# Moving the memory reads of an attention segment to other slots of a hand-written timetable

## The chip, the core and the metric

The kernel runs on one core of one Trainium2 chip. The metric is the device time of one execution in microseconds (us). All times here are in us unless marked ns.

A core has a matrix engine (TensorE, PE in the profile, its weight loads PEld), a vector engine (VectorE, DVE), an activation engine (ScalarE, ACT), a general engine (GpSimd, POOL), and a queue that issues transfers (SyncE, SP). Each runs its own instructions in order and waits for others on semaphores. Matrix products are written to PSUM; VectorE or ScalarE takes them out again, which is called evacuation below.

## The reference

Two branches share one layer norm of `x` (2048 tokens, 640 features) and are multiplied at the end.

```python
xn = layernorm(x)
# branch A: attention with a memory, 32 heads of 20, 4 segments of 512 tokens
q, k, v = heads(xn @ wq), heads(xn @ wk), heads(xn @ wv)
M, z = 0, 0
for s in range(4):
    p     = softmax(q_s @ k_s.T * scale + causal_mask)
    a_dot = p @ v_s
    a_mem = (phi(q_s) @ M) / (phi(q_s) @ z + 1e-6)       # the memory read
    o_s   = g * a_mem + (1 - g) * a_dot                  # g = sigmoid(beta)
    M     = M + phi(k_s).T @ v_s
    z     = z + phi(k_s) summed over tokens
s = concat(o) @ wo
# branch B: a gated unit of width 1536
h = sigmoid(xn @ w_gate) * (xn @ w_up)
out = x + s * silu(h @ w_down)
```

Here `phi(t)` is `t + 1` for positive `t` and `exp(t)` otherwise. The memory read of a segment uses the memory `M`, `z` of the segments before it, so the first segment (n = 0) has none.

## The kernel before

**Slots.** The work is cut into 80 slots, 20 for each segment n, numbered here 0 to 79; segment n has slots 20n to 20n+19. A slot begins with the scores of one unit of attention (`scores`, line 548, tile `Sps`, four banks of PSUM) and the exponential of these on ScalarE (`exps`, line 556, tile `pt`, then masked by GpSimd). The rest of the slot is filled with other matrix products.

**What fills a slot.** Two sorts of work fill it. The dense queue holds, in order, the gate products (`gp`, `do_gate`), the up products (`up`, `do_up`) and the down products (`yp`, `do_down`) of branch B. They are generators: a gate or up product is 5 pieces of 512 columns, a down product 12 pieces of 320, and the filler takes piece after piece. The other sort are events with due times, from the table `TIMES`, in slots from the segment's start: memory reads (`mem_part`, tile `am`, 8 in a segment from n = 1 on), output products (`out_mm`, tile `sp`), projections for the next segment (`psq`, `psv`), layer norm, transfers. The time's whole part names the slot, and its fraction the place in the slot's free time. If more than two products of events fall into one open dense product, that one is run to its end first (`inside`, line 921):

```python
            if ns > 0:
                inside[0] += 1
                if inside[0] > 2:
                    complete()
```

**Two forms of a product.** All of these products go through `mm` (lines 130 and 134). It issues either one matmul over 128 columns of weights (line 130), or four over 32 columns each, side by side in the array (line 134). The second form is chosen for the slots whose end has a product of attention with values (`attend_T`, line 572, tile `ApsT`), which is itself in 32-column tiles. These are the slots that come just before a "visit":

```python
        ORDER["columns"] = slot + 1 in visits
```

In a segment these are the slots 0, 3, 5, 8, 10, 13, 15 and 18 from its start. So slots 23, 25, 28 and 30 use the 32-column form in segment 1, and 22, 24, 26, 27 and 29 the 128-column form.

**A memory read.** `mem_part(n, j, half)` multiplies 128 tokens of phi(q) (`qtd`) with the memory (`Mbd`), in three pieces of 147, 147 and 84 columns (or in another order), and VectorE evacuates it in three instructions: line 413 (`rm`), line 415 (its reciprocal) and line 416 (`odot`). The reads of a segment must be done before their result is spilled (`mem_spill`, 11.56 slots after the segment's start).

**PSUM buffers.** Besides `Sps` there are four buffers, from one pool, `ps_d`, for all other products. A product's tile takes a buffer when the code reaches it, in the recorded order, and its first matmul waits until the product that had the buffer before is evacuated. The evacuations are: `gp` by a tanh on ScalarE (line 427, tile `tg`), `up` by VectorE (line 438, tile `hT`, which also needs `tg`), `yp` by a tanh on ScalarE (line 454) and then VectorE (line 455, tile `aa`), `sp` by VectorE (line 499, then line 502 adds to `xt` after every second one), `am` by VectorE as above, `ApsT` by a transpose on VectorE (line 593, tile `tb`). The `hT` tiles are the weights of the down products.

VectorE also does the layer norm of the next segment (lines 240, 241, 249), the transposes of the attention's result (line 591, tile `obT`) and phi (lines 366, 367, 375, with an exponential on ScalarE, line 371).

## Time and profile before

| | |
|---|---|
| median of 3 runs | 319.95 us (319.74 to 320.09) |
| span of the profiled execution, first to last instruction | 317.6 us |
| whole time of the profiled execution | not listed apart from the three runs; 2.35 us lie between its span and the median |
| granted TensorE clock, mean | 0.999 |
| busy: TensorE, VectorE, ScalarE, GpSimd | 309.7, 229.5, 227.2, 135.5 us |
| slots 22 to 29, from `Sps` to `Sps` | 109.53 to 137.14 us of the span |
| slots 42 to 49 | 175.94 to 202.90 us |
| slots 62 to 69 | 242.22 to 268.74 us |

In the timeline view a row is a run of equal instructions: start, length, engine, line, operation, output and inputs, shape, count, and in brackets the engine's idle time before it with what ended it. The records of matmuls overlap: each shows its way through the array, so one product's cost to TensorE is read from its start to the start of the next. Some matmul records are missing, so a count can be one short.

### The profile page before, as it was taken

How to read it: one execution, taken by the hardware profiler on the slowest of the kernel's cores; microseconds unless marked ns; L12 is line 12 of the kernel's file. 1: busy time of each engine (PE TensorE's matmuls, PEld its weight loads, DVE VectorE, ACT ScalarE, POOL GpSimd, SP SyncE). 2: the span in 40 equal slices, each digit the busy share in tenths (PEclk: the TensorE clock that was granted, in tenths of full speed). 3: DMA queues.
4: the chain of work that ended last, by engine and by line, in shares of the span. 5: the costliest groups of instructions: out<-in, count | busy, mean ns of one | idle time of the engine just before them, and what ended most of it. 6: DMA issues, size and time to landing. Idle time of an engine off the chain costs nothing.

```text
span 317.6 us, 10049 instructions
## 1 busy us (share of the span) xinstructions
PE 309.7 (98%) x4215; PEld 167.1 (53%) x4244; DVE 229.5 (72%) x505; ACT 227.2 (72%) x229; POOL 135.5 (43%) x230
## 2 busy tenths in 40 slices
PE   8999999999999999999999999999999999999995
PEld 3544445665555445654665455545466645445673
DVE  6474356755869888997779999977787686734565
ACT  3723477788898877778898868678897766777631
POOL 1870036535263445334453354444533353535322
PEclk9999999999999999999999999999999999999999
DMA  7984886420752462505954443238533000350302
GB/s 252 364 328 142 289 221 191 105 46 2 215 158 62 130 130 85 126 23 173 240 168 122 114 110 109 82 121 210 168 82 120 19 23 23 114 137 4 99 20 83
DMA packets 56085, 41.36 MB, mean 130 GB/s; under 512 B 26952, under 2 KB 54664, under 8 KB 56040
## 3 DMA queue, kind: packets, MB, share of 16 engines
q1 hardware_dynamic: 53496, 35.97, 39.7%
q10 hardware_dynamic: 2544, 4.75, 4.0%
q8 instruction: 33, 0.54, 0.7%
q14 instruction: 12, 0.10, 0.1%
HBM read 19.90 MB, written 14.78 MB: 109 GB/s over the span
## 4 chain that ended last, share of the span: by engine, by line
PE 96%; issue 1%; ACT 1%; DVE 1%; ACTq 0%
PE yp L130 11%; PE up L130 11%; PE gp L130 10%; PE psq L130 10%; PE Sps L548 9%; PE gp L134 6%; PE up L134 6%; PE yp L134 6%; PE psv L130 6%; PE ApsT L572 5%; PE psq L134 4%; PE sp L130 3%; PE sp L134 3%; PE sp L532 2%; PE psv L134 1%; PE wps L644 1%
## 5 line engine op out<-in xcount | busy, mean ns | idle before, releaser
L556 ACT ACTIVATE pt<-Sps 128x2048 bf16<-128x2048 f32 (+1 forms) x81 | 150.3, 1856 | 40.8 <-PE Sps L548 35.9
L558 POOL TENSOR_SCALAR_AFFINE_SELECT pt<-pt 128x512 bf16<-128x512 bf16 x128 | 83.2, 665 | 157.6 <-ACT pt L556 157.5
L438 DVE SCALAR_TENSOR_TENSOR hT<-tg,up 128x512 bf16<-128x512 bf16 x48 | 32.4, 675 | 23.2 <-PE up L130 8.7
L130 PE MATMUL up<-xnT,Wu 128*128 128x512 bf16 x147 | 40.3, 380 | 1.2 <-issue 1.0
L130 PE MATMUL yp<-Wd,hT 128*128 128x320 bf16 x257 | 40.1, 300 | 0.0
L427 ACT ACTIVATE tg<-gp 128x512 bf16<-128x512 f32 x48 | 28.6, 596 | 14.4 <-PE gp L130 11.0
L130 PE MATMUL gp<-xnT,Wg 128*128 128x512 bf16 x144 | 38.1, 379 | 0.3 <-issue 0.2
L548 PE MATMUL Sps<-QT,KT 23*128 23x128 bf16 (+3 forms) x512 | 32.6, 301 | 0.2
L591 DVE STREAM_TRANSPOSE obT<-ob 128x512 bf16<-128x512 bf16 x30 | 21.1, 705 | 13.4 <-POOL ob L587 13.3
L130 PEld LDWEIGHTS <-hT 128*128 128x128 bf16 x257 | 23.5, 98 | 11.6 <-issue 3.0
L455 DVE SCALAR_TENSOR_TENSOR aa<-t,yp 128x320 bf16<-128x320 bf16 x32 | 15.3, 480 | 13.8 <-ACT t L454 13.7
L134 PE MATMUL gp<-xnT,Wg 128*32 128x512 bf16 x360 | 24.1, 380 | 0.0
L548 PEld LDWEIGHTS <-KT 23*128 23x128 bf16 x512 | 10.0, 92 | 24.5 <-issue 24.1
L130 PEld LDWEIGHTS <-Wu 128*128 128x128 bf16 x160 | 14.3, 98 | 16.2 <-issue 3.2
L593 DVE STREAM_TRANSPOSE tb<-ApsT 128x512 f32<-128x512 f32 x30 | 21.2, 708 | 2.2 <-PE ApsT L572 2.1
L572 PE MATMUL ApsT<-pt,V 128*32 128x512 bf16 (+2 forms) x480 | 22.7, 299 | 0.0
L130 PEld LDWEIGHTS <-Wg 128*128 128x128 bf16 x150 | 14.1, 98 | 16.0 <-issue 1.9
L134 PE MATMUL up<-xnT,Wu 128*32 128x512 bf16 x320 | 21.7, 380 | 0.0
L454 ACT ACTIVATE t<-yp 128x320 bf16<-128x320 f32 x32 | 13.9, 435 | 10.2 <-PE yp L130 8.5
L130 PE MATMUL psv<-Wv,xnT 128*128 128x320 bf16 x130 | 20.6, 299 | 0.2
L587 POOL TENSOR_TENSOR ob<-tb,rb 128x320 bf16<-128x320 f32 x27 | 19.8, 733 | 2.3
L134 PE MATMUL yp<-Wd,hT 128*32 128x320 bf16 x508 | 20.0, 300 | 0.0
(122 smaller groups left out, 448.7 us busy)
## 6 DMA issues: line engine op xcount, KB each, us to landing
KT<-Kd SPq DMA_DIRECT2D x32, 80.0 KB
QT<-Qd SPq DMA_DIRECT2D x32, 80.0 KB
out_dram<-xt SPq DMA_DIRECT2D x14, 160.0 KB
Wg<-in_B_w_gate_dram ACTq DMA_DIRECT2D x1, 1920.0 KB
Wu<-in_B_w_up_dram ACTq DMA_DIRECT2D x1, 1920.0 KB
xt<-in_A_x_dram SPq DMA_DIRECT2D x3, 640.0 KB
Wd<-in_B_w_down_dram SPq DMA_DIRECT2D x1, 1920.0 KB
Xd<-xn SPq DMA_DIRECT2D x12, 160.0 KB
```

The source lines that it names most:

```text
L130: nc.tensor.matmul(out_, lhsT=lhsT, rhs=rhs, start=start, stop=stop, skip_group_check=True)
L134: nc.tensor.matmul(out_[cols], lhsT=lhsT[:, cols], rhs=rhs, start=start, stop=stop, tile_position=(0, 32 * r), skip_group_check=True)
L427: nc.scalar.activation(tg[:], gp[:], ACT.Tanh, scale=0.5)
L438: nc.vector.scalar_tensor_tensor(out=h[:], in0=seg[n]["tg"][:], scalar=1.0, in1=up[:], op0=ALU.add, op1=ALU.mult)
L455: nc.vector.scalar_tensor_tensor(out=s["aa"][j][:, hs], in0=t2[:], scalar=1.0, in1=yp[:], op0=ALU.add, op1=ALU.mult)
L548: nc.tensor.matmul(Sps[:, r, c0:c0 + ncol], lhsT=KT[32 * r:32 * r + DH + 3, g, kb * P:(kb + 1) * P], rhs=QT[32 * r:32 * r + DH + 3, g, q0: ...
L556: nc.scalar.activation(pt[:, :, 0:ntot], Sps[:, :, 0:ntot], ACT.Exp, scale=SCALE)
L558: nc.gpsimd.affine_select(out=pt[:, :, c0:c0 + P], in_=pt[:, :, c0:c0 + P], compare_op=ALU.is_ge, fill=0.0, base=0, pattern=[[0, 4], [1, P ...
L572: nc.tensor.matmul(ps[32 * r:32 * r + 32, q0:L], lhsT=Vflat[n % 2][:, off:off + 32], rhs=t[:, r, c0:c0 + ncol], start=(i == 0), stop=(i == ...
L587: nc.gpsimd.tensor_tensor(ob[:, :, 0:DH], tb[:, :, 0:DH], rb[:].unsqueeze(2).to_broadcast([P, L // 32, DH]), op=ALU.mult)
L591: nc.vector.transpose(s["obT", g // 4][:, g % 4, :], ob[:].rearrange("p b e -> p (b e)"))
L593: s["turn", g] = (lambda: nc.vector.transpose(tb[:].rearrange("p b e -> p (b e)"), ps[:]), quotients, turn_back)
```

## The change

Only the due times of the eight memory reads of a segment are changed, in the timetable (line 66):

```diff
-    update=-1.6, mem=(2.1, 3.8, 3.0, 6.1, 7.0, 2.3, 9.0, 10.0), mem_spill=11.56, mem_T=14.4,
+    update=-1.6, mem=(3.03, 3.45, 3.85, 5.15, 5.6, 8.15, 8.6, 10.0), mem_spill=11.56, mem_T=14.4,
```

Before, a segment's reads lie in the slots 2, 2, 3, 3, 6, 7, 9 and 10 from its start, three of them in slots of the 32-column form. Afterwards they lie in 3, 3, 3, 5, 5, 8, 8 and 10, all of them slots of the 32-column form. The filler puts dense pieces where the reads were and takes them from where the reads go.

## The prediction

> **What bounds the kernel now.** I read the page first: the busy shares, then the chain that ended last.

> ```profile
> PE 309.7 (98%) x4215; PEld 167.1 (53%) x4244; DVE 229.5 (72%) x505; ACT 227.2 (72%) x229; POOL 135.5 (43%) x230
> ...
> PE 96%; issue 1%; ACT 1%; DVE 1%; ACTq 0%
> ```

> TensorE is busy 98% of the span, and 96% of the chain is TensorE, spread over all its products. So whatever leaves TensorE working without a hole costs nothing, and each hole made in its stream goes onto the end time in full. Two questions remain: does a memory read (am) take TensorE longer in 32-column form, and do the moved reads make it wait?

> The timeline of TensorE, segment 1, slots 22 (its end) and 23 answers the first. Ends overlap in these records, so I read cost as start to next start.

> ```profile
> 111.29 1.24 PE L130 MATMUL gp<-xnT,Wg 128*128 128x512 bf16 x5
> 112.37 0.38 PE L130 MATMUL up<-xnT,Wu 128*128 128x512 bf16 x1
> 112.68 0.40 PE L548 MATMUL Sps<-QT,KT 23*128 23x512 bf16 x4
> 113.01 0.35 PE L134 MATMUL am<-Mbd,qtd 128*32 128x147 bf16 x12
> 113.18 1.04 PE L134 MATMUL up<-xnT,Wu 128*32 128x512 bf16 x16
> ```

> A piece of gp or up costs 1.08/5 = 0.22; Sps x4 0.32; an am in 32-column form (x12) 0.17. In 128-column form, x3 from 110.31 to 110.48, it is 0.17 as well. By the same reading a sp product is 0.68, a yp piece 0.14, ApsT 0.65, Sps x8 0.34.

> The second question needs ACT and VectorE. Segment 2, slot 45 (its Sps starts at 185.82), the timeline of ACT:

> ```profile
> 186.32 1.88 ACT L556 ACTIVATE pt<-Sps 128x2048 bf16<-128x2048 f32 x1 [0.43 <-PE Sps L548]
> 188.10 0.59 ACT L427 ACTIVATE tg<-gp 128x512 bf16<-128x512 f32 x1
> ```

> The exponential starts 0.50 after the slot does and holds ACT until 2.28. A tanh of a gate product finished inside the slot therefore ends at 2.87 at the earliest, however early that product is done. Segment 1, slot 28 (from 129.25), the timeline of VectorE:

> ```profile
> 127.85 0.48 DVE L366 TENSOR_SCALAR mn<-ktok 128x1280 bf16<-128x1280 bf16 x1
> 128.37 0.97 DVE L367 TENSOR_SCALAR ktok<-ktok 128x1280 bf16<-128x1280 bf16 x1
> 129.26 0.47 DVE L499 TENSOR_TENSOR aa<-aa,sp 128x320 bf16<-128x320 bf16 x1
> 129.66 0.70 DVE L591 STREAM_TRANSPOSE obT<-ob 128x512 bf16<-128x512 bf16 x1
> 130.29 0.64 DVE L438 SCALAR_TENSOR_TENSOR hT<-tg,up 128x512 bf16<-128x512 bf16 x1
> 130.86 0.80 DVE L375 TENSOR_TENSOR ktok<-ktok,mn 128x1280 bf16<-128x1280 bf16 x1
> 131.59 0.47 DVE L499 TENSOR_TENSOR aa<-aa,sp 128x320 bf16<-128x320 bf16 x1
> 132.09 0.59 DVE L502 TENSOR_TENSOR xt<-aa,xt 128x640 bf16<-128x640 bf16 x1
> 132.61 0.47 DVE L455 SCALAR_TENSOR_TENSOR aa<-t,yp 128x320 bf16<-128x320 bf16 x1
> 133.00 0.47 DVE L499 TENSOR_TENSOR aa<-aa,sp 128x320 bf16<-128x320 bf16 x1
> ```

> No idle time stands between these rows: in this slot VectorE is the fuller engine, although its share of the whole span is 72%. Here TensorE already loses a little: the sp at 130.13 lasts to 130.99, 0.86 where 0.68 is its cost.

> **The change, part by part.** Only the order inside slots 22 to 29, 42 to 49 and 62 to 69 differs. Of the 24 reads, 9 are in 32-column form now; afterwards all 24 are, so 15 change form. As built, slots hold 3 reads (23, 43, 63), 2 (25, 45, 65), 2 (28, 48, 68) and 1 (30, 50, 70, as now). The dense pieces displaced go to neighbouring slots; the number of products stays.

> *TensorE's own work.* 15 reads at 0.17 against 15 at 0.17, dense pieces at 0.22 in both forms (gp x20 in 32 columns, 114.05 to 115.13, is 1.08): sum 0. Switches of form stand around Sps as before: 0. The 90 more matmuls and loads are inside the 0.17.

> *Queues.* SP, POOL and ACT keep their instructions in the same order, and no DMA is moved past another. VectorE keeps its 24 evacuations (rm, reciprocal, odot: 110.79 to 111.68, 0.89 each), in other places. So all of the cost is waiting for the four PSUM buffers that products share. In the built order each product's buffer tells whose evacuation it waits for. I walk the tight places with rows of before, as offsets from the slot's start, and add 0.05 from a release to the matmul (estimate; ACT follows the gp ending at 112.53 by 0.04).

> *Slot 45.* New order: gp 1, am, gp 1, sp, gp 1, am, up. The second am is the third insertion into an open gp, which forces that gp to its end; then up gets gp's own buffer. up wants to start at 0.32+0.22+0.17+0.22+0.68+0.22+0.17 = 2.00; the tanh ends at 2.87. Wait 0.9. In before, two sp stood there and up had another buffer. Behind the waiting up, sp and ApsT are queued, and everything after them. Nothing hides this.

> *Slot 43* (exponential at +0.51, tanh ends at 2.87 too): gp 1, am, gp 3, up 1, am, up 4, am, and the next gp takes the first gp's buffer at 0.32+0.22+0.17+0.65+0.22+0.17+0.86+0.17 = 2.78. Wait 0.15. *Slot 23*: ApsT is the one that takes gp's buffer, at 3.0 by the same addition: covered, by 0.1; 0.25 if that margin goes.

> *Slot 28.* New order: yp 2, am, yp 1, sp, yp 1, yp' 1, sp', am', yp' 4, ApsT. VectorE: obT at 0.41, hT 1.04 to 1.68 as in before, then am's evacuation from 1.61 to 2.59, the ktok addition from 2.50, sp's aa 3.23 to 3.70, xt from 3.73, yp's aa 4.25 to 4.72. TensorE: the last yp piece needs hT as weights at 0.32+0.27+0.17+0.14+0.68 = 1.58, waits 0.15. sp' wants to start at 2.0 in am's buffer, free at 2.59: waits 0.6. am' wants sp's buffer at 2.64+0.68 = 3.32, free at 3.70: waits 0.45. ApsT wants yp's buffer at 3.75+0.17+0.54 = 4.46, free at 4.72: waits 0.3. Together 1.5; slot 28 of before already loses 0.18, so 1.3.

> *Slot 48* has the same pattern with gp in yp's place. sp' wants am's buffer at 2.04. If VectorE is as late as in before (obT done at 1.75), am is evacuated at 2.73: wait 0.75, and ApsT loses 0.25 more. If it is early, since slots 46 and 47 have each lost a read (0.89 of VectorE), nearly no wait: 0.1. I take the middle, 0.45; the row nearest to it, obT at 196.79, speaks for the upper end, the relief for the lower.

> *What is gained.* Slot 49 starts without a read: its waits of before, 0.1, go; so does the 0.1 in slot 27 (a sp behind hT). Segment 3: VectorE idles 1.0 to 1.4 at a time at 252 to 266 and covers its moved reads: 0; the price without that cover is about slot 48's, 0.5.

> Sum: 0.9+0.15+1.3+0.45-0.2 = 2.6. The profiled execution has a span of 317.6; its own whole time isn't among the times, so I take the 2.35 between span and the median 319.95 as what lies around, unchanged. 319.95+2.6 = 322.6 (span 320.2).

> [...]

> **The rivals.** *Evacuations keep up.* If no product meets a busy buffer, only gains are left: the losses of before in these slots, 0.11 (27), 0.18 (28), 0.10 (49), 0.08 (63, 70 together), give 319.5; with 15 reads 0.01 cheaper each (some of the 128-column ones take 0.177 against 0.165) 319.3. This is the side that isn't slower. It decides at slot 45: the tanh would have to end by 2.00, and the exponential before it ends only at 2.28. Against it: two fixed durations. For it: nothing but the cover seen in segment 3.

> *The backlog spreads.* VectorE, behind after slots 28 and 48, makes slots 23, 65 and 68 wait as well: 2.6 + 0.25 + 0.5 + 0.5 for slot 48's upper end = 3.9, that is 323.9. For it: slots 25 and 65 reuse a read's buffer with only some 0.4 to spare. Against it: every wait of TensorE gives VectorE time to catch up.

> *Reads bound by their weight loads.* If several reads in one slot run at load pace, 3 loads of 97 ns one after the other in each column group (that row is the LDWEIGHTS from qtd), each read costs 0.29 instead of 0.17: 15 x 0.12 = 1.8 more, 324.4. [...] Against it: the x12 rows.

> **How the numbers follow.** Forecast (waits as walked, some more or less) 0.77; evacuations keep up 0.07; backlog spreads 0.13; load pace 0.03. About 0.2% (0.64) is what a measurement of this kernel can tell from no change. Slower by more: 0.77+0.13+0.03, less a little for walked waits that come out at a quarter, 0.91; the keep-up case is 0.06 same and 0.03 faster at its edge. Low end: slot 45 at 0.85, slot 28 at half, the rest nothing, less 0.2, is +1.3, 321.2. High end: the spread case and 0.3 over, 324.2.

> **What would show it.** Right: in slot 45 a hole of 0.9 ahead of up, put down to ACT tg; in slot 28 some 1.5 of holes ahead of L134 sp, am and ApsT, put down to DVE odot and aa; am groups x12 still 0.17; the span from the Sps of slot 22 to that of slot 30 longer by about 1.2 and of slots 42 to 50 by 1.4, of 62 to 70 the same. Wrong: no holes at these places, am groups longer than 0.2, or holes in slots 31 to 41, where nothing is moved.

## The result and the profile after

The changed kernel takes 321.59 us where the kernel before takes 319.92: a ratio of 1.005, 95% interval 1.0034 to 1.0066. That is the median of three executions (321.24 to 321.72); a fourth, the profiled one, ran at a granted clock of 0.66 and took 451.29, and with it the median is 321.65. A second measurement, `after_again`, gave 322.04 against 319.65, 1.0074 (1.0051 to 1.0096). It is slower, as forecast: by 1.7 in the first measurement and 2.4 in the second, where the forecast was 2.65. All profile lines "of after" below are of `after_again`, whose profiled execution took 321.68 with a span of 319.9, 2.3 more than the span before.

The page, its first busy line and the first line of the chain that ended last:

```profile
PE 313.0 (98%) x4334; PEld 166.8 (52%) x4334; DVE 228.5 (71%) x505; ACT 227.0 (71%) x229; POOL 135.1 (42%) x230
...
PE 91%; DVE 5%; issue 1%; ACT 1%; DMA 1%; DVEq 0%; ACTq 0%
```

The busy shares say nothing: TensorE is at 98% as before. The chain does: 5% of it is VectorE now, where it was 1%. TensorE waits for evacuations.

What a read costs TensorE did not change. The timeline of TensorE in slot 23:

```profile
113.29 0.34 PE L134 MATMUL am<-Mbd,qtd 128*32 128x147 bf16 x12
113.45 0.39 PE L134 MATMUL up<-xnT,Wu 128*32 128x512 bf16 x4
113.67 0.82 PE L134 MATMUL gp<-xnT,Wg 128*32 128x512 bf16 x12
114.32 0.34 PE L134 MATMUL am<-Mbd,qtd 128*32 128x147 bf16 x12
114.48 0.39 PE L134 MATMUL gp<-xnT,Wg 128*32 128x512 bf16 x4
```

From start to next start both reads take 0.16, where the load-pace rival has 0.29.

Slot 45 begins at 187.03. The timeline of ScalarE, then that of TensorE:

```profile
187.53 1.88 ACT L556 ACTIVATE pt<-Sps 128x2048 bf16<-128x2048 f32 x1 [0.43 <-PE Sps L548]
189.31 0.59 ACT L427 ACTIVATE tg<-gp 128x512 bf16<-128x512 f32 x1
```

```profile
188.64 0.39 PE L134 MATMUL gp<-xnT,Wg 128*32 128x512 bf16 x4
189.02 0.35 PE L134 MATMUL am<-Mbd,qtd 128*32 128x84 bf16 x12
189.95 0.62 PE L134 MATMUL up<-xnT,Wu 128*32 128x512 bf16 x8 [0.58 <-ACT tg L427]
```

The tanh ends at 189.90, 2.87 after the slot's start, and the up product follows 0.05 later, as the prediction has it. From gp to am 0.38 passes where 0.22 is the cost, and from am to up 0.93 where it is 0.17: 0.16 and 0.76 are lost. The wait of 0.16 ahead of am, which the walk did not have, is VectorE's (an hT that ends at 188.96). It adds nothing, since up has to wait for the tanh in any case.

Slot 28 begins at 129.13. The timeline of VectorE, to be set against the ten rows of the prediction:

```profile
128.97 0.70 DVE L591 STREAM_TRANSPOSE obT<-ob 128x512 bf16<-128x512 bf16 x1
129.59 0.64 DVE L438 SCALAR_TENSOR_TENSOR hT<-tg,up 128x512 bf16<-128x512 bf16 x1
...
130.64 0.49 DVE L416 TENSOR_TENSOR odot<-am,rm 128x320 bf16<-128x320 f32 x1
131.05 0.82 DVE L375 TENSOR_TENSOR ktok<-ktok,mn 128x1280 bf16<-128x1280 bf16 x1
131.78 0.48 DVE L499 TENSOR_TENSOR aa<-aa,sp 128x320 bf16<-128x320 bf16 x1
132.30 0.49 DVE L502 TENSOR_TENSOR xt<-aa,xt 128x640 bf16<-128x640 bf16 x1
132.71 0.48 DVE L455 SCALAR_TENSOR_TENSOR aa<-t,yp 128x320 bf16<-128x320 bf16 x1
```

VectorE takes up obT 0.16 before the slot begins; before the change it did so 0.41 after. The rows that follow hold the distances that the prediction walked: each is 0.56 to 0.59 earlier than in the walk, and the last one 0.67.

Where the 2.3 us went. What a slot loses is its length from `Sps` to `Sps` less the work that it holds, at the costs that the prediction reads; lengths alone can't be compared, since dense pieces have moved between slots. The table has the loss less that of before. Slots that hold the same work in both kernels agree within 0.03 unless they are named here:

| slots | forecast | measured |
|---|---|---|
| 45 | +0.9 | +0.94 |
| 43 | +0.15 | +0.16 |
| 28 | +1.3 | +0.69 |
| 48 | +0.45 | +0.19 |
| 23 | 0 (0.25 if the margin goes) | +0.07 |
| 27 and 49 | -0.2 | -0.12 and -0.10 |
| 62 to 69 | 0 | +0.09 |
| 50 | none | +0.06 |
| **38** | none; "wrong" by the prediction's own list | **+0.41** |

The slots 22 to 29 together, from `Sps` to `Sps`, are longer by 0.64 where about 1.2 was forecast, 42 to 49 by 1.18 for 1.4, and 62 to 69 by 0.09 for none.

Nothing is moved in slot 38, and the order of its work is the same in both kernels. Its rows on TensorE's timeline, after:

```profile
164.39 0.82 PE L391 MATMUL dm<-V,ktok 128*32 128x63 bf16 x80
165.01 1.55 PE L134 MATMUL yp<-Wd,hT 128*32 128x320 bf16 x40
166.79 0.73 PE L572 MATMUL ApsT<-pt,V 128*32 128x512 bf16 x16 [0.23 <-issue]
```

and before:

```profile
163.79 0.82 PE L391 MATMUL dm<-V,ktok 128*32 128x63 bf16 x80
164.42 1.55 PE L134 MATMUL yp<-Wd,hT 128*32 128x320 bf16 x40
165.78 0.73 PE L572 MATMUL ApsT<-pt,V 128*32 128x512 bf16 x16
```

From the yp to ApsT it is 1.78 instead of 1.36. The idle time is put down to "issue": no semaphore that the profile knows ended it.

### The profile page after: what moved, and what is told of

The parts are those of the page before. It is cut to its first block, busy times and chain, and to the rows that moved or that the text cites. A ratio compares the mean times of both kernels' runs of the same rounds, so it can differ in the third digit from the quotient of the medians.

```text
span 449.6 us, 10228 instructions
## 1 busy us (share of the span) xinstructions
PE 439.5 (98%) x4305; PEld 201.1 (45%) x4334; DVE 236.0 (52%) x505; ACT 231.2 (51%) x229; POOL 134.3 (30%) x230
## 4 chain that ended last, share of the span: by engine, by line
PE 97%; issue 1%; DVE 1%; DMA 1%; ACT 0%
PE yp L130 12%; PE up L130 12%; PE gp L130 11%; PE psq L130 10%; PE Sps L548 7%; PE gp L134 6%; PE psv L130 6%; PE ApsT L572 6%; PE yp L134 6%; PE up L134 6%; PE psq L134 4%; PE sp L130 3%; PE sp L134 3%; PE sp L532 2%; PE psv L134 1%; PE am L134 1%
## 5 line engine op out<-in xcount | busy, mean ns | idle before, releaser
L556 ACT ACTIVATE pt<-Sps 128x2048 bf16<-128x2048 f32 (+1 forms) x81 | 150.3, 1855 | 94.0 <-PE Sps L548 93.3
L438 DVE SCALAR_TENSOR_TENSOR hT<-tg,up 128x512 bf16<-128x512 bf16 x48 | 32.8, 683 | 60.9 <-PE up L130 42.5
L130 PE MATMUL up<-xnT,Wu 128*128 128x512 bf16 x153 | 58.5, 504 | 2.1 <-issue 1.8
L130 PE MATMUL yp<-Wd,hT 128*128 128x320 bf16 x263 | 57.5, 382 | 0.0
L130 PE MATMUL gp<-xnT,Wg 128*128 128x512 bf16 x147 | 55.8, 511 | 0.8 <-issue 0.5
L427 ACT ACTIVATE tg<-gp 128x512 bf16<-128x512 f32 x48 | 28.6, 596 | 44.9 <-PE gp L130 30.9
L130 PEld LDWEIGHTS <-hT 128*128 128x128 bf16 x263 | 28.9, 116 | 22.0 <-issue 4.8
L455 DVE SCALAR_TENSOR_TENSOR aa<-t,yp 128x320 bf16<-128x320 bf16 x32 | 15.6, 487 | 40.4 <-ACT t L454 40.4
L548 PE MATMUL Sps<-QT,KT 23*128 23x128 bf16 (+3 forms) x512 | 36.3, 337 | 0.0
L134 PE MATMUL gp<-xnT,Wg 128*32 128x512 bf16 x348 | 34.3, 507 | 0.0
L572 PE MATMUL ApsT<-pt,V 128*32 128x512 bf16 (+2 forms) x480 | 32.2, 391 | 0.0
L130 PEld LDWEIGHTS <-Wg 128*128 128x128 bf16 x153 | 18.1, 123 | 28.0 <-issue 25.9
L130 PEld LDWEIGHTS <-Wu 128*128 128x128 bf16 x166 | 17.3, 114 | 29.2 <-issue 27.6
L130 PE MATMUL psv<-Wv,xnT 128*128 128x320 bf16 x130 | 29.6, 395 | 0.3 <-issue 0.2
L134 PE MATMUL up<-xnT,Wu 128*32 128x512 bf16 x296 | 29.1, 503 | 0.5 <-ACT tg L427 0.5
L130 PE MATMUL psq<-xnT,Wq 128*128 128x512 bf16 x82 | 28.5, 512 | 0.4
L134 PE MATMUL yp<-Wd,hT 128*32 128x320 bf16 x484 | 27.9, 383 | 0.0
L548 PEld LDWEIGHTS <-KT 23*128 23x128 bf16 x512 | 9.5, 92 | 37.5 <-issue 37.5
L591 DVE STREAM_TRANSPOSE obT<-ob 128x512 bf16<-128x512 bf16 x30 | 21.1, 703 | 6.4 <-POOL ob L587 6.4
```

The source lines that it names most:

```text
L130: nc.tensor.matmul(out_, lhsT=lhsT, rhs=rhs, start=start, stop=stop, skip_group_check=True)
L134: nc.tensor.matmul(out_[cols], lhsT=lhsT[:, cols], rhs=rhs, start=start, stop=stop, tile_position=(0, 32 * r), skip_group_check=True)
L427: nc.scalar.activation(tg[:], gp[:], ACT.Tanh, scale=0.5)
L438: nc.vector.scalar_tensor_tensor(out=h[:], in0=seg[n]["tg"][:], scalar=1.0, in1=up[:], op0=ALU.add, op1=ALU.mult)
L455: nc.vector.scalar_tensor_tensor(out=s["aa"][j][:, hs], in0=t2[:], scalar=1.0, in1=yp[:], op0=ALU.add, op1=ALU.mult)
L548: nc.tensor.matmul(Sps[:, r, c0:c0 + ncol], lhsT=KT[32 * r:32 * r + DH + 3, g, kb * P:(kb + 1) * P], rhs=QT[32 * r:32 * r + DH + 3, g, q0: ...
```

## The experiments

The theory of the prediction is that all of the loss is waiting for evacuations, each at its place. Two things were open: whether the places and prices add up, and what slot 38 is.

### The parts of the change, each alone

Each kernel takes the changed due times of one slot of the segment and leaves the other reads as before; the changed kernel ran beside them.

```diff
 # only_slot5
-    update=-1.6, mem=(2.1, 3.8, 3.0, 6.1, 7.0, 2.3, 9.0, 10.0), ...
+    update=-1.6, mem=(2.1, 3.8, 3.0, 5.15, 5.6, 2.3, 9.0, 10.0), ...
 # only_slot8
+    update=-1.6, mem=(2.1, 3.8, 3.0, 6.1, 7.0, 8.15, 8.6, 10.0), ...
 # only_slot3
+    update=-1.6, mem=(3.03, 3.45, 3.85, 6.1, 7.0, 2.3, 9.0, 10.0), ...
```

> The changed kernel once more, for a profile at the full granted clock. Theory W (waits for PSUM buffers): about 1.7 to 2.6 us over before, with holes of 0.9 us in slot 45 ahead of up, 0.15 us in slot 43, 1.3 us more than before in slot 28, up to 1.0 us in slot 48, and nothing in slots 31 to 41 and 51 to 61. Rival P (pace of the weight loads): the am groups of twelve take 0.29 us from start to next start instead of 0.17, and the loss lies in every slot that has such a group, segment 3 included. Rival K (evacuations keep up): no holes, the span as before.

> Only the two reads of the slot 5 from the segment's start are moved there (from 6 and 7). W: the hole in slot 45 is there in full, 0.9 us; slots 28 and 48 are as in before; some 0.4 us may come up in slot 25, where sp now follows two reads; together +0.9 to +1.4 us. P: two more reads in 32-column form in each of three segments, 6 x 0.12 = +0.7 us, equally in all three. K: 0.

> Only the two reads of the slot 8 are moved there (from 2 and 9). W: slot 28 loses 1.3 us more than before, slot 48 loses 0.5 to 1.0 us, slot 45 nothing, segment 3 nothing: +1.5 to +2.3 us. P: 6 x 0.12 = +0.7 us, equally in all three segments. K: 0.

> Only the reads of slot 3 are placed as in the changed kernel (3.03, 3.45, 3.85); one read stays in slot 2. W: a small loss, 0.15 us in slot 43, some tenths elsewhere where the dense pieces have slid: 0 to +0.7 us. P: one more read in 32-column form in each segment, 3 x 0.12 = +0.36 us. K: 0.

| | median | before | ratio (95%) | what its slots show |
|---|---|---|---|---|
| all (`after_again`) | 322.04 | 319.65 | 1.0074 (1.0051 to 1.0096) | table above |
| `only_slot5` | 321.63 | 319.65 | 1.0060 (1.0037 to 1.0082) | 45 +0.73, 25 +0.52, 28 -0.19, 39 +0.46 |
| `only_slot8` | 322.62 | 319.65 | 1.0096 (1.0068 to 1.0123) | 28 **+1.75**, 48 +0.54, 39 **+1.11** |
| `only_slot3` | 321.95 | 319.65 | 1.0069 (1.0047 to 1.0092) | 63 +1.10, 23 +0.59, 48 +0.26, 45 +0.24 |

All three came out dearer than expected. `only_slot5` lost 2.0 for 0.9 to 1.4 and `only_slot8` 3.0 for 1.5 to 2.3; of these, 0.46 and 1.11 are holes in slot 39, which are taken up with slot 38 below. `only_slot3` lost 2.3 for 0 to 0.7, and the 0.15 expected in its slot 43 did not come. Its slots 45 and 48 lose 0.24 and 0.26, though none of its moved reads lies there: in slot 48 VectorE takes up obT 1.50 after the slot begins, where it was 1.11 before the change.

So the parts do not add up: 2.0, 3.0 and 2.3 make 7.3, and the whole costs 2.4 (5.7 and 2.0 without the holes of slots 38 and 39). A read that is taken out of one slot gives VectorE 0.89 for the next. `only_slot5` takes the reads out of slots 26 and 27 and puts none into slot 28, which begins at 129.66. VectorE takes up obT 0.39 before that, and the slot loses nothing any more (-0.19):

```profile
129.27 0.70 DVE L591 STREAM_TRANSPOSE obT<-ob 128x512 bf16<-128x512 bf16 x1
```

The opposite case is slot 28 of `only_slot8`, which begins at 129.21 with the reads of slots 26 and 27 still ahead of it. The timeline of VectorE:

```profile
129.31 0.47 DVE L499 TENSOR_TENSOR aa<-aa,sp 128x320 bf16<-128x320 bf16 x1
129.71 0.70 DVE L591 STREAM_TRANSPOSE obT<-ob 128x512 bf16<-128x512 bf16 x1
...
131.79 1.21 DVE L375 TENSOR_TENSOR ktok<-ktok,mn 128x1280 bf16<-128x1280 bf16 x1
132.92 0.48 DVE L499 TENSOR_TENSOR aa<-aa,sp 128x320 bf16<-128x320 bf16 x1
```

and that of TensorE:

```profile
131.03 0.46 PE L134 MATMUL yp<-Wd,hT 128*32 128x320 bf16 x8
131.93 0.86 PE L134 MATMUL sp<-Wo,oT 128*32 128x320 bf16 x20 [0.44 <-DVE odot L416]
133.45 0.35 PE L134 MATMUL am<-Mbd,qtd 128*32 128x84 bf16 x12 [0.66 <-DVE aa L499]
```

Here obT begins 0.50 after the slot, close to the 0.41 that the prediction assumed, and the price is 1.75: the 1.3 of the forecast, and 0.4 for the ktok addition that takes 1.21 instead of 0.80. All four waits of the walk are there, sp' at 2.72 for 2.64 and am' and ApsT 0.4 to 0.5 later than walked, behind that addition. So the walk of slot 28 was right and its starting point was not: in the whole change the reads of slots 26 and 27 have left, and VectorE is early.

The row of slot 45 that matters comes out alike in `only_slot5` (its slot begins at 186.54): ScalarE's timeline

```profile
188.82 0.59 ACT L427 ACTIVATE tg<-gp 128x512 bf16<-128x512 f32 x1
```

ends at 189.41, again 2.87 after the start, and up starts at 189.46. In `only_slot3` two of the three slots with three reads pay (23 and 63). ApsT stands still there, and the view puts its wait down to VectorE's rows for the reads; TensorE's timeline in slot 63:

```profile
251.34 0.73 PE L572 MATMUL ApsT<-pt,V 128*32 128x512 bf16 x16 [0.67 <-DVE rm L413]
```

In the whole change the same three reads in slot 63 cost 0.09. There six, five and three pieces of the down product follow the reads, and in `only_slot3` seven, seven and two. VectorE sits idle for 0.89 just ahead of the first of these reads in `only_slot3`, so the read that stays in slot 62 is not what it is late with. Why the two differ so much was not shown.

### The exponential of slot 45 cut to half

In the changed kernel the exponential of slot 45 covers half of its columns, and GpSimd fills the rest.

```diff
-    def exps(unit):
+    def exps(unit, short=False):
...
-        nc.scalar.activation(pt[:, :, 0:ntot], Sps[:, :, 0:ntot], ACT.Exp, scale=SCALE)
+        nexp = ntot // 2 if short else ntot
+        nc.scalar.activation(pt[:, :, 0:nexp], Sps[:, :, 0:nexp], ACT.Exp, scale=SCALE)
+        if short:
+            nc.gpsimd.memset(pt[:, :, nexp:ntot], 0.0)
...
-        pts[slot] = exps(unit)
+        pts[slot] = exps(unit, slot == 45)
```

> The changed kernel, with the exponential of slot 45 alone taken over half of its columns (the other half is set to zero by GpSimd, so this slot's attention is left incomplete). Theory W (up waits in slot 45 for the tanh of the gate product whose buffer it gets): the tanh no longer queues behind the exponential, so the hole shrinks from 0.94 us; it can't go, since the gate product itself ends only 0.17 us before up wants to start, and 0.16 of latency and 0.59 of tanh follow: about 0.65 us is left. If VectorE or a transfer holds up there, the hole stays at 0.94 us.

It took 322.56 against 319.71, 1.0088 (1.0071 to 1.0104): no gain as a whole. 1.29 of the loss in its profile is a hole in slot 38, which is taken up below. Its slot 45 begins at 187.72. ScalarE's timeline:

```profile
188.22 1.02 ACT L557 ACTIVATE pt<-Sps 128x1024 bf16<-128x1024 f32 x1 [0.42 <-PE Sps L548]
189.77 0.60 ACT L427 ACTIVATE tg<-gp 128x512 bf16<-128x512 f32 x1 [0.52 <-DVE rm L413]
```

TensorE's:

```profile
189.33 0.39 PE L134 MATMUL gp<-xnT,Wg 128*32 128x512 bf16 x4
...
190.42 0.62 PE L134 MATMUL up<-xnT,Wu 128*32 128x512 bf16 x8 [0.36 <-ACT tg L427]
...
192.20 0.51 PE L575 MATMUL ApsT<-pt,V 128*32 128x512 bf16 x8 [0.49 <-DVE aa L499]
```

With the exponential short, the tanh no longer stands behind it: it starts at 189.77, 0.05 after the gate product's last matmul ends (189.72; the view puts the wait down to a VectorE row, the last event before it). The up product follows the tanh, 0.05 after its end, and starts 2.70 after the slot instead of 2.92. So up waits for the tanh and the tanh for the exponential, and behind that stands the gate product itself. The hole ahead of up shrinks by 0.22, to 0.72 where about 0.65 was expected. But slot 45 as a whole loses 1.39 now, 0.45 more than in after. What takes the gain back stands beside the fill on GpSimd: while its MEMSET runs (190.63 to 191.58) a VectorE row ahead of the aa that ApsT waits for takes 1.29, where the same instruction takes 0.44 in the same slot of after. GpSimd is busy beside it there too, with ob and the select, so that the MEMSET makes the difference is likely but not shown:

```profile
190.47 1.29 DVE L249 TENSOR_SCALAR xn<-xt,mv,rs 128x640 bf16<-128x640 bf16 x1
191.68 0.47 DVE L499 TENSOR_TENSOR aa<-aa,sp 128x320 bf16<-128x320 bf16 x1
```

### Reads evacuated by one instruction

In the changed kernel each read's evacuation is one VectorE instruction instead of three; the division by the normalizer is left out.

```diff
-        rm = opool.tile([P, 16], F32, name="rm", bufs=3)
-        nc.vector.scalar_tensor_tensor(out=rm[:], in0=am[:, :, DH], scalar=1e-6, ...)
-        nc.vector.reciprocal(rm[:], rm[:])
...
-            am[:, :, 0:DH], rm[:].unsqueeze(2).to_broadcast([P, 16, DH]), op=ALU.mult)
+            am[:, :, 0:DH], ginv[:, 16 * half:16 * half + 16].unsqueeze(2).to_broadcast([P, 16, DH]), op=ALU.mult)
```

> The changed kernel with each read evacuated by one VectorE instruction instead of three (the division by the normaliser is left out, the product with the gate stays): 0.41 us of VectorE a read instead of 0.89. W: slots 28 and 48, where VectorE is the late one, lose at most 0.2 us more than before each (0.69 and 0.19 in the changed kernel); slots 43 and 45, where ScalarE's tanh is awaited, keep 0.16 and 0.94 us. If the loss came from the 32-column form of the reads itself, all of these would stay.

It took 321.00 against 319.71, 1.0044 (1.0026 to 1.0062). Slot 48 lost nothing (0.19 in after) and slot 43 kept its 0.16, as the theory has it. Slot 28 still lost 0.46 over before, where at most 0.2 was expected. TensorE's timeline shows what is left:

```profile
133.05 0.73 PE L568 MATMUL ApsT<-pt,V 128*32 128x512 bf16 x16 [0.32 <-DVE aa L451]
```

sp' and am' are nearly free of waits; ApsT still waits for the down product's aa, which stands behind xt and the ktok addition in VectorE's queue and not behind a read alone. Slot 45 lost 0.51, where 0.94 was expected to stay. That was a miss on the order: here the tanh holds up the sp behind up, and not up, so gp's buffer has gone to that sp. The tanh ends at 2.87 again, and what waits for it starts 0.05 later again.

The same run holds the longest hole of all in slot 38, 2.66 us longer than before, on TensorE's timeline:

```profile
166.19 0.38 PE L568 MATMUL ApsT<-pt,V 128*32 128x512 bf16 x1
168.86 0.72 PE L568 MATMUL ApsT<-pt,V 128*32 128x512 bf16 x15 [2.29 <-issue]
```

One matmul of a product has run and its fifteen sisters wait. A buffer would be waited for by the first of them.

### Slot 38: instructions added ahead of everything

The page of before has a queue that carries instructions:

```profile
q8 instruction: 33, 0.54, 0.7%
```

```diff
 # before_pad80: the kernel before, 80 TensorE instructions more
-    keep_warm(9)
+    keep_warm(7)
+    for i in range(42):
+        c = slice(32 * (i % 4), 32 * (i % 4) + 32)
+        nc.tensor.matmul(wps[c, 0:32], lhsT=warm[:, c], rhs=warm[:, 0:32], start=True, stop=True,
+                         tile_position=(0, 32 * (i % 4)), skip_group_check=True)
 # after_pad130: the changed kernel, the same with range(67), 130 more
```

> The timetable of before, no read moved; only TensorE's stream is 80 instructions longer at its start: 42 tiny warm-up matmuls of 32 columns in place of 2 large ones (84 more matmuls and loads each counted, less 4). Theory F (TensorE's instructions come in blocks of 256, and a block that is used up in about 2.3 us by 32-column code isn't there in time): a hole of 0.3 to 0.7 us comes up in slot 38, where the changed kernel has one, and nothing else in the slots 20 to 79 changes by more than 0.15. Rival S (the hole in slot 38 of the changed kernel is a late effect of its waits in slots 23 to 30): no hole in slot 38.

> The changed kernel with TensorE's stream 130 instructions longer at its start (67 tiny warm-up matmuls in place of 2 large ones). F: the end of a block moves out of the slots 38 and 39, and the hole of 0.41 us there goes; the holes in slots 28, 43, 45 and 48 stay as they are. S: the hole in slot 38 stays.

`before_pad80` took 320.53 against 319.71, 1.0028 (1.0010 to 1.0045). It now has a hole of 0.51 in slot 38, in the midst of the down product. TensorE's timeline:

```profile
165.25 1.26 PE L134 MATMUL yp<-Wd,hT 128*32 128x320 bf16 x30
166.73 0.58 PE L134 MATMUL yp<-Wd,hT 128*32 128x320 bf16 x10 [0.21 <-issue]
```

Its profiled execution has one more hole, of 0.98 in slot 9, that is none of this sort. It was ended by a transfer:

```profile
68.73 1.25 PE L130 MATMUL psq<-xnT,Wk 128*128 128x512 bf16 x5 [0.81 <-DMA xnT<-Xd]
```

`after_pad130` took 321.43 against 319.71, 1.0054 (1.0039 to 1.0069). The hole of slot 38 is gone; TensorE's timeline goes from yp to ApsT in 1.36, as before the change:

```profile
165.11 1.55 PE L134 MATMUL yp<-Wd,hT 128*32 128x320 bf16 x40
166.47 0.73 PE L572 MATMUL ApsT<-pt,V 128*32 128x512 bf16 x16
```

Slots 28, 43, 45 and 48 lose 0.68, 0.16, 0.94 and 0.19, what they lose without padding. The intervals of after with and without it overlap, so the times alone don't show the 0.41; the traces do.

The trace's records of queue q8 complete it. The block ahead is counted as the 256 instructions ahead of that place (128 loads and 128 matmuls), by the estimate above, and each row has the q8 transfer of the time in which they run; that it brings the block which begins at the place is the theory's part. `spread_reads` is the kernel of the next section:

| kernel | TensorE enters the block ahead | transfer | TensorE goes on in the new block | after the transfer's end |
|---|---|---|---|---|
| before (no hole) | 163.93 | 164.59 to 165.94 | 167.62 | 1.68 |
| `only_slot3` (no hole) | 164.98 | 165.48 to 166.46 | 167.89 | 1.43 |
| after | 163.99 | 164.61 to 165.57 | 166.79 | 1.22 |
| `only_slot5` | 164.05 | 164.73 to 165.79 | 167.13 | 1.34 |
| `only_slot8` | 165.59 | 166.95 to 167.83 | 169.30 | 1.47 |
| `exp_half45` | 163.79 | 165.11 to 166.16 | 167.48 | 1.32 |
| `before_pad80` | 163.82 | 164.31 to 165.25 | 166.73 | 1.48 |
| `reads_1op` | 163.80 | 164.80 to 167.59 | 168.86 | 1.27 |
| `spread_reads` | 163.93 | 163.92 to 165.23 | 166.55 | 1.32 |

Wherever there is a hole, it ends 1.2 to 1.5 after the transfer does, whether that took 0.9 or 2.8. In before the block lasts 3.7, because its end lies in the 128-column products of slot 39; in after, shifted by the reads' extra instructions, it is all 32-column code and is used up in 2.4 (163.99 to 166.79 without the hole of 0.41). In `only_slot3` it lasts 2.9, and there is no hole.

### All reads in 32-column form, without the collisions

```diff
 # spread_reads, against the kernel before
-    update=-1.6, mem=(2.1, 3.8, 3.0, 6.1, 7.0, 2.3, 9.0, 10.0), ...
+    update=-1.6, mem=(3.1, 8.73, 0.07, 10.74, 3.39, 8.32, 0.31, 10.13), ...
 # spread_pad130: the same, and the padding of after_pad130
```

> All 24 reads stay in slots of the 32-column form, as in the changed kernel, but two at a time and early in their slots: in the slots 0, 0, 3, 3, 8, 8, 10 and 10 from the segment's start (mem = 3.1, 8.73, 0.07, 10.74, 3.39, 8.32, 0.31, 10.13). Slot 45 has none. Theory (the form costs nothing, what costs is the collision of a read with a busy buffer): the walk of the order gives at most some +0.6 of waits against the kernel before (0.5 of it in slot 27), nothing in slots 45 and 48, plus whatever a crossing of TensorE's instruction blocks adds (0 to 1): 319.9 to 321.2. Rival (the 32-column form of a read costs by itself): as many reads are changed in form as in the changed kernel, so it loses as much, 321.6 or more.

> The same placing of the reads, with the first warm-up cut from 9 to 7 and 67 tiny 32-column products put in its place, 130 more TensorE instructions ahead of everything. By the theory of instruction blocks the crossing near slot 38 comes elsewhere: the hole of 0.4 to 0.5 that the changed kernel has there (166.3) is gone, as it was with the same padding on the changed kernel, and what is left over the kernel before is the +0.6 of waits: about 320.2 to 320.6. If the holes in slot 38 come from what the slot waits for (buffers, transfers), the padding moves nothing and both kernels of this call are alike.

`spread_reads` took 321.08 against 319.35, 1.0045 (1.0030 to 1.0061), within the expected 319.9 to 321.2; `spread_pad130` 319.88 against the same, 1.0018 (1.0003 to 1.0032), below the expected 320.2. With as many reads in 32-column form as the changed kernel has, at most 0.3% is left in the padded kernel. The slots 23, 43, 48, 63 and 68 of both hold two such reads each and lose nothing, so the form is not what costs. In slots 42 to 49 both are 0.17 shorter than before. The padding took the hole of slot 38 away once more (from 0.33 to nothing).

The hole alone does not make up the 1.2 between the two medians, and the spans of the two profiled executions differ by only 0.1 (the padded one is among its longer ones, 320.9). Slot 27 loses 0.36 without the padding and 0.71 with it, where 0.5 was walked, and slot 33 0.59 and 0.10; why was not shown. In both profiles slot 53 loses 0.59, and the walk had neither slot 33 nor 53. In slot 53 the next slot's scores wait for the exponential ahead; TensorE's timeline of the padded kernel:

```profile
218.29 0.41 PE L548 MATMUL Sps<-QT,KT 23*128 23x384 bf16 x8 [0.62 <-ACT pt L556]
```

ScalarE was late with it, having waited for VectorE's mn first. Neither kernel beats the one before.

## Why the prediction was right, and where it was not

**Direction and size.** Slower had 0.91, and it is slower; 321.6 lies within 321.2 to 324.2, near the low end. The way to it holds in kind: TensorE's own work did not change, and 1.9 of the 2.3 lost is TensorE waiting for evacuations that are late. The other 0.4 is slot 38, of another kind.

**Slot 45: right.** 0.94 for 0.9, with the hole ahead of up (0.16 of it ahead of am) and ACT's tg named as its end. The two fixed durations (the slot's start to the exponential 0.50, the exponential and the tanh to 2.87) reproduce in three kernels, and halving the exponential frees the tanh. One detail was wrong: no third insertion forces gp to its end there. In the built order two of its pieces lie in slot 44 and three in slot 45, and it ends by itself. The place and the price are the same.

**Slot 43 and the gains: right.** 0.16 for 0.15; -0.12 and -0.10 for -0.2 together.

**Slot 28: the term that failed in size.** The step was "VectorE: obT at 0.41, hT 1.04 to 1.68 as in before". VectorE began obT at -0.16. The relief from reads that leave slots 26 and 27 was counted for slot 48 and not here, though it is the same 0.89 each. By part: sp' lost 0.2 for the 0.6 of the walk, am' 0.45 for 0.45, ApsT 0.22 for 0.3, and the yp piece nothing for 0.15; 0.87 in all, less the 0.18 of before. `only_slot8`, where VectorE is late, shows the walk to be right from the late start: 1.75.

**Slot 48: the upper bound was not reached.** 0.19 for 0.45, between the bounds 0.1 and 1.0. The relief decided it, as the lower end had it: obT began at 197.56, 0.26 before the slot, where it was 1.11 after the slot's start in before.

```profile
197.56 0.70 DVE L591 STREAM_TRANSPOSE obT<-ob 128x512 bf16<-128x512 bf16 x1
```

Not all of that is the two reads. VectorE's mn and ktok rows ahead of it take 0.42 and 0.50, where they took 0.97 and 0.81 in before, and the prediction's relief counted the reads alone.

**Slots 62 to 69: right in kind.** 0.09 for 0.

**What the prediction did not have.** The 0.41 of slot 38 is by its own list a sign against it, and rightly: "so all of the cost is waiting for the four PSUM buffers" and "90 more matmuls and loads are inside the 0.17" left out that more instructions ahead of a place can bring a hole there or take it away: 80 more made one of 0.51 in slot 38 of before, 130 more took the 0.41 of after to nothing. This hole stood in for part of the excess of slot 28, so the total hides an error of a term, and its nearness is in part luck. With slot 28 at its measured 0.69 the forecast would have been 2.0, and the span without the hole grew by 1.9.

**The rivals.** "Evacuations keep up" fell at slot 45, its own test. "Load pace" fell on the x12 rows at 0.16. "The backlog spreads" named slots 23, 65 and 68; in the whole change these lose 0.07, 0 and 0. It shows signs only in the parts alone, where the slots ahead have not been relieved: slot 25 in `only_slot5` and the later obT of slot 48 in `only_slot3`.

## What to carry to other kernels

When work is moved in a schedule, walk the destination with the queues as they are after the departure: the reads that left slots 26 and 27 made the slot that took them half as expensive, and each part of this change alone costs nearly as much as the whole or more (1.5, 1.9 and 2.3 against 2.0, without the holes of slots 38 and 39). Look for the fixed chain that no relief moves (here exponential, then tanh, then the buffer), since that price could be read from the old trace to 0.05 us. A hole that the profile puts down to "issue", at an instruction in the midst of a product, is looked for at the same program count in other builds before it is explained by the change.

## What the runs showed of the hardware that was not expected

**Instruction blocks.** The page of before has 33 transfers of 16 KB on queue q8, which it names "instruction", against 8459 matmuls and weight loads of TensorE: 256.3 for each. That they are blocks of TensorE's program is the author's reading. In a stretch of 32-column products, where the 256 instructions ahead of one place took 2.3 to 2.6 us (table of slot 38, without the holes), TensorE stood still at that place for 0.33 to 2.66 us in seven kernels. The q8 transfer began 0 to 1.4 after the first of these instructions, took 0.9 to 2.8 (in after the transfers of queue q1 take 74% of the DMA engines' time from 163.9 to 166.3), and 1.2 to 1.5 more passed until TensorE went on. There is no hole where the 256 instructions last 2.9 us (`only_slot3`) or 3.7 us (before). The hole at one and the same place differs from kernel to kernel (0.33, 0.41, 0.46, 0.51, 1.11, 1.29, 2.66), with the transfer's start and length and the time that the block ahead lasts; that this also spreads the times of one kernel is likely, but was not shown.

**VectorE beside GpSimd.** Some VectorE instructions took 1.5 to 3 times as long as in other rows while a GpSimd instruction ran: xn 1.29 for 0.44 beside the MEMSET, the ktok addition 1.21 for 0.80 in `only_slot8`, where GpSimd's select runs from 131.69 to 132.32. Over the eleven profiles of before, `after_again` and the nine other kernels, the 92 xn rows with GpSimd idle all took 0.40 to 0.45. Of the 84 beside a GpSimd instruction 60 took the same, and 24 took 0.54 to 1.29. So GpSimd stands beside every long row, but not every row beside GpSimd is long. This was seen in rows side by side and not tested by itself.
